# Fused attention and mixture of experts: the experts' slots are chosen beside the token scatters, with early units of 256 rows, three units of 448 rows and another PSUM order

## The chip, the cores and the metric

The kernel runs on one core of a Trainium2 chip. The metric is the device time of one execution in microseconds; three runs of the kernel before took 967.88, 968.69 and 969.49 us, a median of 968.69. The engines are TensorE (PE, with weight loads as PEld), VectorE (DVE), ScalarE (ACT), GpSimd (POOL) and SyncE (SP). Each has its own instruction queue and takes its instructions in order; they meet through semaphores.

## The reference

```python
# attention: q, k, v of 8 batches x 8 heads x 576 rows x 64
scores = scale * q @ k.T
thresh = max(scores) - tau                      # tau = 0.02
scores = where(scores >= thresh, scores, -1e9)
x = softmax(scores) @ v                         # rows: 4608 tokens x 512
# mixture of 8 experts, one expert per token
logits = x @ w_gate
e_idx = argmax(logits)                          # the token's expert
gate_w = softmax(logits)[e_idx]
eom = sigmoid(x @ w_output_gate)
for e in range(8):
    h = maximum(x[e_idx == e] @ w1[e], 0)       # 512 -> 1024
    out[e_idx == e] = gate_w * eom[:, e] * (h @ w2[e])   # 1024 -> 512
```

All of it is float32. The matmuls of the experts are made in three products of halves: each operand is split into a high part and the remainder (xh, xl; w1h, w1l; w2h, w2l; hh, hl), and hi*hi, hi*lo and lo*hi are summed in PSUM.

## The kernel before, in words

**Attention** (class `Attention`) goes through the batches in pairs, software pipelined over steps g. As soon as a pair's rows of x are known, its logits are summed (`logit_sums`) and a generator `Router.route` is put into a queue. `advance`, called in every step, moves that queue on by a piece. `route` takes the argmax, counts the tokens per expert so far by two matmuls (`place`) and scatters each row of 514 numbers (512 of x, the gate and the token's number) with nine indirect DMAs of 128 rows into a DRAM buffer `xs`, where expert e has its region from row e*CAP. The routing of the last pair can only be done when attention has ended, so it lies beside the first expert work. The rows of the first two experts ("early" experts) that come from the earlier pairs (up to `cut`) go into regions of their own of `esize` rows, so that their units can start before the last pair is routed.

**Experts** (class `Experts`) works in units. A unit is a block of rows of one expert, with eight f steps, each of 128 of the 1024 hidden columns. In a step, `first(f)` makes 12 matmuls of 128x128 weights against all the rows of the unit (lines 945 to 947), ACT makes hh (949), DVE makes hl (950), and `second(f)` makes three matmuls of 512 columns per tile of 128 rows, with the hidden rows as the stationary operand (966 to 968), summed over f in one PSUM bank per tile. `run` emits `first` of a step ahead of `second` of the step before. `finish` scales the sums (751) and writes them by indirect DMA to the tokens' rows of the output (752). The next unit's rows are loaded by `gather` from `xs` (908, on SP's queue), and `prep` transposes them by 64x64 pieces (931) and splits them (761, 764), in two calls during the later steps of the unit ahead.

The weights come in quarters of an expert: SP loads two halves of 512 KB per quarter (`load`, 718) into one of RB = 4 raw buffers; `split_until` makes the high half on ACT (761) and the low half on DVE (764), into NW = 4 sets, some steps ahead of their use.

The order of units in `begin` is: two early units of 384 rows; then six units of 512 rows (experts 2 to 7, `Base`), with four units of 256 rows (`Pair`) between them, whose expert and rows come from a table "p" made on DVE in `Router.finish` after all counts are known; and one unit of 128 rows (`Flex`), interleaved into the eleventh unit and the beginning of the last. Behind everything a loop (`rest`) runs a `Flex` unit for each slot of 128 rows that is left, read from a table "s"; on these inputs nothing was left. Altogether the static units have room for 4992 rows.

Slots are filled with whatever lies in `xs`; rows that no token fills must be harmless. So `finish` scatters pad rows (`zrow`) behind each expert's last row with eight indirect DMAs (`pads`), and `init_units` fills other rows with 32 DMAs during attention. The third unit's gather is held until the token scatters and the pads are done.

PSUM has eight banks. When attention ends, the expert part opens three pools over the banks that attention frees: y (4 banks, the sums), x (2, transposes), h (2, hidden).

Of the kernel before, what the change touches and what calls it, by code (L numbers as in the profile page):

```python
# [20 lines left out]
class Attention:  # L21
# [281 lines left out]

    def run(self, hooks):
# [4 lines left out]
        for g in range(G + self.TAIL):  # L309
# [68 lines left out]
class Router:  # L378
    NPAIR = 4

    def __init__(self, ctx, tc, ntok, E, DM, early, esize, cut):
# [12 lines left out]
        self.A = E * self.CAP + 2 * P  # L394
# [9 lines left out]
        self.ecap = c.tile([P, E], F32, name="ecap")  # L404
        self.asc = c.tile([P, E], F32, name="asc")
# [3 lines left out]
        for e in range(E):  # L409
            nc.gpsimd.memset(self.ebase[:, e : e + 1], float(e * self.CAP + self.base[e]))  # L410
            nc.gpsimd.memset(self.elim[:, e : e + 1], float(e * self.CAP + esize) if e < early else -1.0)
# [19 lines left out]
        self.prows = c.tile([1, 2, self.NPAIR], I32, name="pairs")  # L431
        self.total = c.tile([1, 1], I32, name="total")
        self.odd = ctx.enter_context(tc.tile_pool(name="rodd", bufs=1))
        self.ripe = False
# [14 lines left out]
    def init_units(self):  # L449
        E = self.E  # L450
        parts = [(self.xs[self.A :, :], "itok")]
        for e in range(self.early, E + 1):
            n = self.base[e] if e < E else 2 * P
            parts.append((self.xs[e * self.CAP : e * self.CAP + n, :], "itok"))
        for dst, group in parts:
            for r in range(0, dst.shape[0], P):
# [4 lines left out]
                yield None  # L461
# [23 lines left out]
    def route(self, bp, rows, LX):  # L485
# [77 lines left out]
        G.tensor_copy(rows[:, :, self.DM], sc)  # L563
        yield False
# [30 lines left out]
    def finish(self, ctx):  # L595
        nc, E = self.nc, self.E
        sm = ctx.enter_context(self.tc.tile_pool(name="rfin", bufs=1, reuse_waits="tile"))
        V = nc.vector
        pad = sm.tile([P, E], F32, name="padf")
        padi = sm.tile([P, E], I32, name="padi")  # L600
        V.tensor_scalar(pad, self.cnt, self.pid, None, op0=ALU.add)
        V.tensor_copy(padi, pad)
# [6 lines left out]
        row = lambda n, name, dt=F32: sm.tile([1, n], dt, name=name)  # L609
        ni, nj, nf, np, m0, v = row(E, "ni", I32), row(E, "nj", I32), row(E, "nf"), row(E, "np"), row(E, "m0"), row(E, "v")  # L610
        cp, ci, cm = row(E + 1, "cp"), row(E + 1, "ci"), row(E + 1, "cm")
        V.tensor_tensor(nf, self.cnt[0:1], self.ebase[0:1], op=ALU.subtract)
        V.tensor_scalar(nf, nf, float(P - 1), None, op0=ALU.add)
        V.tensor_copy(ni, nf)
        yield False
# [58 lines left out]
class Experts:  # L674
# [102 lines left out]
    def begin(self, nstatic):  # L777
# [6 lines left out]
        for i in range(len(make)):  # L784
            for g in range(4):
                self.seq.append((i, g))
                if i == self.FLEX:
                    self.seq.append((None, g))
# [377 lines left out]
```

## Time and profile before

| | us |
|---|---|
| median of the runs | 968.69 (967.88 to 969.49) |
| the profiled execution | 967.93 |
| its span | 966.2 |
| attention's last matmuls, first expert matmul | 490.43 |
| first matmul of the third unit | 568.63 |
| first matmul of the last unit | 909.49 |
| last matmul | 958.16 |
| mean granted TensorE clock | 0.995 |

The page of the profile gives the busy time of each engine, the span in 40 slices, and the groups of instructions with what they waited for. A stretch's row gives the busy time of each engine in it, the granted clock as a share of full speed, and the share of the DMA engines. In the timeline each matmul stands with its start and its duration; matmuls are pipelined, so that the distance between starts, not the duration, is what one costs.

### The profile page before, as it was taken

To read this page: it belongs to the slowest core of one execution; us is meant where nothing else is said; L and a number is where in the kernel's file an instruction comes from. 1 tells how busy PE (TensorE), PEld (TensorE's weight loads), DVE (VectorE), ACT (ScalarE), POOL (GpSimd) and SP (SyncE) were. 2 spreads that over 40 slices of the span, in tenths; PEclk is the share of its full clock that TensorE was granted. 3 is DMA by queue.
4 is the path that set the end of the run, shared out by engine and by line. 5 is a ranking of instruction groups with operands and counts; after the bars stand their busy time and mean duration, and the time that the engine had idled before them with its cause. 6 is when DMAs were issued, how large, how long until landed. Compare 5 with 4: busy or idle time off the path is not lost. (4 is left out here: it accounts for less than half of the span.)

```text
span 966.2 us, 22101 instructions
## 1 busy us (share of the span) xinstructions
PE 948.4 (98%) x8491; PEld 716.2 (74%) x8491; DVE 690.3 (71%) x1631; ACT 592.3 (61%) x1052; POOL 339.0 (35%) x573
## 2 busy tenths in 40 slices
PE   9999999999999999999989899999999999999996
PEld 5677676776766767667668787778878878878785
DVE  7999999999999999999865752535535535536721
ACT  6888888888879888788853342324424434435521
POOL 4343443656736675466635410202102002002001
PEclk9999999999999999999999999999999999999998
DMA  4355443133331342317157753426526526537401
GB/s 161 102 165 159 147 151 90 57 93 110 122 93 54 115 132 79 93 54 271 60 188 227 252 180 112 150 90 219 192 84 222 167 89 237 166 98 231 152 11 44
DMA packets 87531, 130.88 MB, mean 135 GB/s; under 512 B 24831, under 2 KB 51711, under 8 KB 87424
## 3 DMA queue, kind: packets, MB, share of 16 engines
q1 hardware_dynamic: 62096, 103.70, 34.1%
q0 software_dynamic: 6640, 21.02, 5.7%
q10 hardware_dynamic: 18688, 4.72, 2.0%
q8 instruction: 68, 1.11, 0.5%
q14 instruction: 39, 0.32, 0.1%
HBM read 95.26 MB, written 30.22 MB: 130 GB/s over the span
## 5 line engine op out<-in xcount | busy, mean ns | idle before, releaser
L162 ACT ACTIVATE p<-s,mn 128x576 f32<-128x576 f32 x288 | 207.7, 791 | 43.2 <-DVE s L148 42.4
L148 DVE TENSOR_SCALAR_CACHE_REDUCE s<-ps 128x576 f32<-128x576 f32 x288 | 205.9, 750 | 26.9 <-PE ps L137 26.3
L175 DVE SCALAR_TENSOR_TENSOR p<-s,thr,p 128x576 f32<-128x576 f32 x288 | 223.5, 812 | 0.0
L137 PE MATMUL ps<-qk 64*128 64x288 f32 (+1 forms) x1280 | 181.7, 419 | 0.1
L949 ACT ACTIVATE hh<-ph 128x512 fp32r<-128x512 f32 (+2 forms) x95 | 48.6, 511 | 208.3 <-PE ph L947 204.1
L155 POOL TENSOR_SCALAR thr<-mn,tau_sb 128x2 f32<-128x2 f32 x144 | 107.1, 744 | 194.9 <-DVE s L148 192.5
L752 POOL DMA_INDIRECT out_dram<-yo,kid x39 | 43.0, 1104 | 367.6 <-DVE yo L751 272.3
L950 DVE SCALAR_TENSOR_TENSOR hl<-ph,hh 128x512 fp32r<-128x512 f32 (+2 forms) x95 | 54.9, 578 | 141.2 <-ACT hh L949 141.1
L945 PE MATMUL ph<-xh,w1h 128*128 128x512 f32 (+2 forms) x380 | 134.7, 354 | 0.6 <-ACT xl L330 0.6
L946 PE MATMUL ph<-xl,w1h 128*128 128x512 f32 (+2 forms) x380 | 132.0, 347 | 0.2 <-DVE xl L764 0.2
L947 PE MATMUL ph<-xh,w1l 128*128 128x512 f32 (+2 forms) x380 | 131.9, 347 | 0.0
L966 PE MATMUL py<-w2h,hh 128*128 128x512 f32 x301 | 119.9, 398 | 3.2 <-ACT hh L949 3.2
L968 PE MATMUL py<-w2h,hl 128*128 128x512 f32 x301 | 119.8, 398 | 3.1 <-DVE hl L950 3.1
L137 PEld LDWEIGHTS ps<-qk 64*128 64x128 f32 (+1 forms) x1280 | 107.5, 177 | 18.4 <-DVE s L148 3.7
L967 PE MATMUL py<-w2l,hh 128*128 128x512 f32 x301 | 119.2, 396 | 0.0
L217 PE MATMUL pt<-ident,p 64*128 64x64 f32 x2304 | 100.9, 227 | 0.0
L239 PE MATMUL pa<-PTb,vld 128*64 128x320 f32 x640 | 100.0, 442 | 0.2 <-DMA PTb<-PTc 0.2
L217 PEld LDWEIGHTS pt<-ident,p 64*128 64x128 f32 x2304 | 82.8, 139 | 19.5 <-issue 13.2
L764 DVE TENSOR_TENSOR w1l<-r,w1h 128x1024 fp32r<-128x1024 f32 x52 | 63.6, 1223 | 23.3 <-ACT w1h L761 22.4
L945 PEld LDWEIGHTS ph<-xh,w1h 128*128 128x128 f32 x380 | 71.3, 188 | 11.9 <-ACT xl L330 0.8
L239 PE MATMUL pa<-PTa,vld 128*64 128x256 f32 x640 | 79.7, 387 | 0.2 <-ACT PTb L202 0.2
L946 PEld LDWEIGHTS ph<-xl,w1h 128*128 128x128 f32 x380 | 71.4, 188 | 10.1 <-DVE xl L764 0.6
(221 smaller groups left out, 1502.3 us busy)
## 6 DMA issues: line engine op xcount, KB each, us to landing
r<-in_moe_w_dram SPq DMA_DIRECT2D x104, 512.0 KB, 3.9
qk<-in_qkv_dram SPq DMA_DIRECT2D x31, 608.0 KB, 4.6
vld<-in_qkv_dram SPq DMA_DIRECT2D x32, 320.0 KB, 4.4
xs<-zrow SPq DMA_DIRECT2D x32, 257.0 KB, 2.7
xg<-xs SPq DMA_DIRECT2D x6, 1028.0 KB
PTb<-PTc ACTq DMA_DIRECT2D x16, 288.0 KB, 4.7
xg<-xs SPq DMA_DIRECT2D x4, 514.0 KB, 4.3
xg<-xs SPq DMA_DIRECT2D x2, 771.0 KB
```

Of the source, the lines that this page charges most:

```text
L137: nc.tensor.matmul(ps[a][rows, o : o + HS], q[pp, t * P : t * P + w], k[pp, k0 : k0 + HS], start=True, stop=True)
L148: nc.vector.tensor_scalar(s, ps[a][:, c0 : c0 + S], SC, None, op0=ALU.mult, op1=ALU.min, accum_out=mn[:, a : a + 1])
L162: self.nc.scalar.activation(e, s, AF.Exp, bias=mn[:, a : a + 1], scale=-1.0)
L175: nc.vector.scalar_tensor_tensor(e, s, thr[:, a : a + 1], e, op0=ALU.is_le, op1=ALU.mult, accum_out=acc[:, a : a + 1])
L217: nc.tensor.transpose(pt[:, o : o + 64], p[hs[h], k0 : k0 + P], id_[hs[h], hs[h]])
L239: nc.tensor.matmul(pa[self.half[a], 0:N], vm[:, kb, a], PT[:, 4 * a + kb if i else self.NK - 1], start=(i == 0), stop=(i == self.NB), skip ...
L945: nc.tensor.matmul(ph, w1h[:, c, fs], self.xh[:, c, 0:N], start=(c == 0), stop=False)
L946: nc.tensor.matmul(ph, w1h[:, c, fs], self.xl[:, c, 0:N], start=False, stop=False)
L947: nc.tensor.matmul(ph, w1l[:, c, fs], self.xh[:, c, 0:N], start=False, stop=(c == 3))
L966: nc.tensor.matmul(Y, hh[:, ts], wh, start=(f == 0), stop=False)
L967: nc.tensor.matmul(Y, hh[:, ts], wl, start=False, stop=False)
L968: nc.tensor.matmul(Y, hl[:, ts], wh, start=False, stop=(f == 7))
```

## The change

1. **Early units of 256 rows** in place of 384 (`esize` is 2 * P).
2. **Slots by size.** The units behind the early ones have fixed sizes: SLOTS = 448, 448, 448, 512, 512, 512, 384, 256, 256, 256, 256, worked in the order UNITS. Which expert and which rows a slot takes is chosen at run time by `choose`, slot by slot: the expert with the most rows left among those whose need, padded, lies at or above the slot's size. With the two early ones that is 13 units with room for 4800 rows. `Flex` has no static place any more; `rest` begins its loop at slot 0.
3. **`choose` stands beside the scatters.** It is a generator in a second queue, moved on by `aside` in each f step, 11 small DVE instructions per slot. A unit's weight loads are issued only when its slot is chosen (`known`).
4. **Units of 448 rows are `Turned`**: in `second` the weights are the stationary operand, the rows stream, so the sum is the transpose, 4 blocks of 128 columns x 448 rows. `finish` copies it to SBUF, and `flip` in steps 1 and 2 of the next unit turns it back with 8 transposes of 128x128 each and writes the rows out.
5. **The third unit's gather does not wait for the pads**: rows up to SAFE = 512 of each region are filled in advance (40 DMAs, two per step of the queue), and pads of rows below that are dropped by an index beyond the bounds.
6. The last pair's two logit sums go through the queue (`last_sums`) instead of standing in line; `advance` is called 6 times a step while the last pair is routed, and none at the very first step; one half split fewer is made ahead in unit 0.
7. The PSUM pools are opened in the order y, h, x.

Of the diff, long parts are left out:

```diff
@@ Attention.run
                 if lu == self.nu - 1:
-                    self.logit_sums(0)
-                    self.logit_sums(1)
+                    rt.queue.append(self.last_sums())
@@ Router
-    NPAIR = 4
+    SLOTS = (448, 448, 448, 512, 512, 512, 384, 256, 256, 256, 256)
+    SAFE = 512
...
+    def aside(self, n):
+        for _ in range(n):
+            if self.side and next(self.side[0], self.side) is self.side:
+                self.side.pop(0)
...
         G.tensor_copy(rows[:, :, self.DM], sc)
+        if bp == self.cut + 1:
+            self.side.append(self.choose())
+            self.last = True
         yield False
...
+    def choose(self):
...
+        for k, z in enumerate(self.SLOTS):
+            yield
+            V.scalar_tensor_tensor(key, st[:, 1], float(z), st[:, 0], op0=ALU.is_ge, op1=ALU.mult)
+            V.tensor_reduce(mx, key, axis=AX.X, op=ALU.max)
+            V.scalar_tensor_tensor(cand, key, mx, self.desc[0:1], op0=ALU.is_equal, op1=ALU.mult)
+            V.tensor_reduce(cm, cand, axis=AX.X, op=ALU.max)
+            yield
...
+            self.tables.append(k)
@@ Router.finish
-        V.tensor_copy(padi, pad)
+        V.tensor_tensor(held, pad, self.first, op=ALU.subtract)
+        V.tensor_scalar(held, held, float(self.SAFE), float(1 << 20), op0=ALU.is_lt, op1=ALU.mult)
+        V.tensor_tensor(padi, pad, held, op=ALU.add)
@@ Experts
-    PAIRS = (2, 4, 6, 8)
-    FLEX = 10
+    UNITS = (0, 3, 7, 1, 8, 4, 9, 2, 6, 10, 5)
...
-        for name, bufs in (("y", 4), ("x", 2), ("h", 2)):
+        for name, bufs in (("y", 4), ("h", 2), ("x", 2)):
...
+        make = [lambda e=e: Base(self, e) for e in range(rt.early)]
+        make += [lambda s=s: (Turned if rt.SLOTS[s] % P else Pair)(self, s) for s in self.UNITS]
+        self.known = lambda i: i < rt.early or self.UNITS[i - rt.early] in rt.tables
...
     def load_next(self):
-        if self.nload < len(self.seq):
+        while self.nload < min(len(self.seq), self.nsplit + self.RB):
             i, g = self.seq[self.nload]
+            if not self.known(i):
+                return
@@ Experts.run
-                if i == self.FLEX and f % 2:
-                    self.flex.step(f // 2, self.take())
...
+                if i and f in (1, 2):
+                    self.unit(i - 1).flip(f - 1)
-                self.split_until(2 * self.used + (4 if f % 2 else 3))
+                self.split_until(2 * self.used + (4 if f % 2 else 3) - (i == 0))
...
-                for _ in range(4):
+                for _ in range(6 if rt.last else 3 if i or f else 0):
                     rt.advance(True)
+                rt.aside(1 if rt.tables and i < rt.early else 2 if i else 4)
+                self.load_next()
@@ Pair
+        rt.after(ins, [x for _, x in rt.tok])
+        if self.s == 0:
+            rt.tc.declare_no_dep(ins.ins, group="pad", reason="rows of their own")
+        else:
+            rt.after(ins, rt.pads)
@@ Turned(Pair)
+    def second(self, f):
...
+        for c, Y in enumerate(self.Y):
+            wh, wl = (w[:, f % 2, c * P : c * P + P] for w in (w2h, w2l))
+            nc.tensor.matmul(Y[:, 0:N], wh, hh[:, 0:N], start=(f == 0), stop=False)
+            nc.tensor.matmul(Y[:, 0:N], wh, hl[:, 0:N], start=False, stop=False)
+            nc.tensor.matmul(Y[:, 0:N], wl, hh[:, 0:N], start=False, stop=(f == 7))
...
+    def flip(self, k):
+        ex, nc = self.ex, self.nc
+        for i, pt in enumerate(ex.px()):
+            t = 2 * k + i
+            o = max(0, t * P - 64)
+            for c in range(4):
+                nc.tensor.transpose(pt[:, c * P : c * P + P], self.yt[:, c, o : o + P], ex.ident)
+            ex.emit_out(pt, self.keys, t, slice(0, P if t else 64))
@@ the call
-        rt = Router(ctx, tc, out.shape[0], w1.shape[0], out.shape[1], 2, 3 * P, nbp - 2)
+        rt = Router(ctx, tc, out.shape[0], w1.shape[0], out.shape[1], 2, 2 * P, nbp - 2)
```

On DVE, in the sixth step of unit 0, the kernel before has this order (r are raw weights, w2l and w1l their low halves, xl the rows' low half, padf and padi the pads' indices; the tables come behind):

```order
L950 SCALAR_TENSOR_TENSOR hl<-ph,hh 128x384
L764 TENSOR_TENSOR xl<-px,xh 128x2x3x64 x2
L764 TENSOR_TENSOR w2l<-r_8062,w2h 128x1024
L950 SCALAR_TENSOR_TENSOR hl<-ph,hh 128x384
L764 TENSOR_TENSOR xl<-px,xh 128x2x3x64 x2
L764 TENSOR_TENSOR w1l<-r_8310,w1h 128x1024
L601 TENSOR_SCALAR padf<-pr,pid 128x8
L602 CAST padi<-padf 128x8
L950 SCALAR_TENSOR_TENSOR hl<-ph,hh 128x384
```

The kernel after has, from the same step on (dst and dsti are the last pair's row numbers for the scatters, st, key, cand and got the choice's state):

```order
L978 SCALAR_TENSOR_TENSOR hl<-ph,hh 128x256
L805 TENSOR_TENSOR xl<-px,xh 128x2x2x64 x2
L805 TENSOR_TENSOR w1l<-r_8078,w1h 128x1024
L560 TENSOR_REDUCE dst<-pso 128x9
L576 CAST dsti<-dst 128x9
L623 TENSOR_TENSOR st<-pr,first 1x8
L624 TENSOR_SCALAR st<-st 1x8
L625 TENSOR_SCALAR st<-first 1x8
L626 COPY st<-asc 1x8
L629 SCALAR_TENSOR_TENSOR key<-st 1x8
L630 TENSOR_REDUCE mx<-key 1x1
L631 SCALAR_TENSOR_TENSOR cand<-key,mx,desc 1x8
```

The row numbers stand ahead of these rows in the kernel before (behind the hl of the third step), and behind the split of the sixth step now, with the choice directly after them and ahead of the next hl.

On SP, around the third unit's gather, the kernel before has (r are halves of weights, xg the unit's rows):

```order
L718 DMA r_8809<-in_moe_w_dram 128x4x256 [waits DMAHW2_49,DVE_49]
L908 DMA xg<-xs 128x4x514 [waits DMASW4_49,DMASW3_49,DMASW5_49,DMASW2_49,DMASW6_49,DMASW1_49,DMASW7_49,DMASW0_49,DMAHW3_49,PE_49,Pool_49]
L718 DMA r_8810<-in_moe_w_dram 128x2x512 [waits DMAHW4_49,DVE_49]
L988 TENSOR_LOAD pairs [waits DVE_49]
L988 ISA x2
L718 DMA r_8905<-in_moe_w_dram 128x4x256 [waits DMAHW5_49,DVE_49]
```

The kernel after has there:

```order
L759 DMA r_8855<-in_moe_w_dram 128x4x256 [waits DMAHW4_49,DVE_49]
L1020 TENSOR_LOAD picks
L1020 ISA x2
L759 ISA
L759 DMA r_8856<-in_moe_w_dram 128x2x512 [waits DMAHW5_49,DVE_49]
L1037 ISA
L1037 DMA xg<-xs 128x3x514 [waits DMASW4_49,DMASW3_49,DMASW5_49,DMASW2_49,DMASW6_49,DMASW1_49,DMASW7_49,DMASW0_49,DMAHW6_49,PE_49,Pool_49]
L1037 ISA
L1037 DMA xg<-xs 64x514 [waits DMAHW7_49]
L1037 ISA
L1037 DMA xg<-xs 64x514 [waits DMAHW0_49]
```

The gather is three transfers now (384 rows, and 64 rows twice, once for each half of the partitions), behind weights of a chosen expert, whose loads wait for the table on DVE.

On TensorE, at a step of a unit of 512 rows behind a turned one, the eight transposes stand between two steps of the kernel after:

```order
L996 MATMUL py<-w2h,hl 128x512
L1104 MATMUL px<-ident,rows 128x128 x8
L973 MATMUL ph<-xh,w1h 128x512
L974 MATMUL ph<-xl,w1h 128x512
L975 MATMUL ph<-xh,w1l 128x512
```

The kernel before goes from the second matmuls of one step directly to the first ones of the next there.

## Rows read from the trace of the kernel before

**Rows 1.** The page: the span.

```profile
span 966.2 us, 22101 instructions
```

**Rows 2.** Busy time by stretches: start:end, length, each engine (x instructions), clock, DMA share, GB/s.

```profile
490.43:568.63 78.20, 72.07 (x408) 62.56 (x406) 50.28 (x121) 29.73 (x46) 29.73 (x41) 0.98 0.64 207
568.63:909.49 340.86, 339.66 (x1842) 278.78 (x1840) 166.43 (x207) 138.64 (x211) 37.14 (x49) 1.00 0.50 164
503.20:506.60 3.40, 3.19 (x8) 2.52 (x9) 2.84 (x6) 2.63 (x5) 0.77 (x3) 0.51 0.65 224
514.00:526.00 12.00, 12.00 (x78) 10.21 (x77) 5.29 (x8) 4.65 (x9) 7.82 (x10) 1.00 0.87 281
530.00:545.00 15.00, 14.40 (x74) 12.87 (x72) 10.84 (x49) 3.67 (x6) 10.67 (x11) 1.00 0.87 295
```

**Rows 3.** Waits of TensorE, 490 to 570: total us, times, longest.

```profile
PE py L966 <- ACT hh L949: 3.2, 2, 2.1
PE py L968 <- DVE hl L950: 2.3, 1, 2.3
PE ph L945 <- ACT xl L330: 0.6, 1, 0.6
```

**Rows 4.** Timeline of TensorE, a step's first matmul: start, us, operation.

```profile
511.40 0.34 PE L945 MATMUL ph<-xh,w1h 128*128 128x384 f32 x1
...
515.58 0.34 PE L945 MATMUL ph<-xh,w1h 128*128 128x384 f32 x1
...
590.83 0.40 PE L945 MATMUL ph<-xh,w1h 128*128 128x512 f32 x1
...
596.42 0.40 PE L945 MATMUL ph<-xh,w1h 128*128 128x512 f32 x1
...
670.69 0.28 PE L945 MATMUL ph<-xh,w1h 128*128 128x256 f32 x1
...
673.49 0.28 PE L945 MATMUL ph<-xh,w1h 128*128 128x256 f32 x1
```

**Rows 5.** The same, around units of 256 rows without and with the flexible unit.

```profile
801.04 0.28 PE L945 MATMUL ph<-xh,w1h 128*128 128x256 f32 x1
...
826.61 0.40 PE L945 MATMUL ph<-xh,w1h 128*128 128x512 f32 x1
...
830.79 0.40 PE L945 MATMUL ph<-xh,w1h 128*128 128x512 f32 x1
...
871.14 0.28 PE L945 MATMUL ph<-xh,w1h 128*128 128x256 f32 x1
...
909.49 0.40 PE L945 MATMUL ph<-xh,w1h 128*128 128x512 f32 x1
...
916.42 0.40 PE L945 MATMUL ph<-xh,w1h 128*128 128x512 f32 x1
```

**Rows 6.** Timeline, flexible unit's transposes and the next matmul; then durations (ns) of all four.

```profile
875.74 0.63 PE L1025 MATMUL px<-ident,xgf 128*128 128x128 f32 x4 [0.22 <-DMA xgf<-xs]
876.12 0.37 PE L945 MATMUL ph<-xh,w1h 128*128 128x256 f32 x1
...
L1025 PE MATMUL px<-ident,xgf x4: 272/273/300, 875.7 to 876.1; 128*128 128x128 f32 x4
```

**Rows 7.** Groups on VectorE, 490 to 570: busy us, mean ns, idle before.

```profile
L764 DVE TENSOR_TENSOR w2l<-r,w2h 128x1024 fp32r<-128x1024 f32 x9 | 11.0, 1221 | 1.9 <-ACT w2h L761 1.9
...
L950 DVE SCALAR_TENSOR_TENSOR hl<-ph,hh 128x384 fp32r<-128x384 f32 x15 | 8.3, 552 | 11.9 <-ACT hh L949 11.8
...
L639 DVE TENSOR_TENSOR cp<-cp,np 1x1 f32<-1x1 f32 x8 | 1.2, 147 | 0.2
```

**Rows 8.** Landing of weights; then token scatters and gathers: duration, first and last start.

```profile
DMA to landing us min/median/max: 5.0/5.8/6.5
...
L473 POOL DMA_INDIRECT xs<-rows,dsti x9: 969/977/1889, 511.3 to 522.8; - x9
...
L908 SPq DMA_DIRECT2D xg<-xs x2: 130/248/367, 544.7 to 568.8; - x2
```

More of the change, by code (lines that the diff above doesn't have):

```diff
@@ L302, in logit_sums, with last_sums @@
             rt.queue.append(rt.route(bp, rt.xrows[bp], LX))
+    def last_sums(self):
+        yield True
+        for k in range(2):
+            self.logit_sums(k)
+            yield True
     def run(self, hooks):
@@ L410, in __init__ @@
             nc.gpsimd.memset(self.ebase[:, e : e + 1], float(e * self.CAP + self.base[e]))
+            nc.gpsimd.memset(self.first[:, e : e + 1], float(e * self.CAP + (self.base[e] if e < early else 0)))
             nc.gpsimd.memset(self.elim[:, e : e + 1], float(e * self.CAP + esize) if e < early else -1.0)
@@ L451, in init_units @@
         parts = [(self.xs[self.A :, :], "itok")]
-        for e in range(self.early, E + 1):
-            n = self.base[e] if e < E else 2 * P
-            parts.append((self.xs[e * self.CAP : e * self.CAP + n, :], "itok"))
+        for e in range(E + 1):
+            r0 = e * self.CAP + (self.base[e] if e < self.early else 0)
+            parts.append((self.xs[r0 : r0 + self.SAFE, :], "itok"))
         for dst, group in parts:
@@ L834, in run @@
                     b.w[f // 2] = self.take()
-                if i == self.FLEX + 1 and f == 1:
-                    self.flex.second(turned)
-                    self.flex.finish()
                 if not ahead:
@@ L848, in run @@
                     prev = (b, f)
-                if i == self.FLEX and f % 2:
-                    self.flex.step(f // 2, self.take())
-                if i == self.FLEX + 1 and f == 0:
-                    turned = self.flex.transposed()
                 k = f - (6 if late else 5)
@@ L860, in run @@
                     self.unit(i + 1).gather()
-                if i == self.FLEX - 1 and f == 7:
-                    self.flex.gather()
-                if i == self.FLEX and f == 0:
-                    self.flex.prep()
                 if rt.pending is not None:
@@ L982, in finish @@
             self.ex.emit_out(Y, self.keys, t)
+    def flip(self, k):
+        pass
 def where(ex, table, s):
@@ L993, in __init__ @@
     def __init__(self, ex, s):
-        self.ex, self.nc = ex, ex.nc
-        self.nt = 2
-        assert "p" in ex.rt.tables
-        self.e, self.row = where(ex, ex.rt.prows, s)
-        self.reset()
-    def gather(self):
-        rt = self.ex.rt
-        self.xg = self.ex.gp.tile([P, 4, rt.W], F32, name="xg")
-        src = rt.xs[bass.ds(self.row, self.N), :]
-        ins = self.nc.sync.dma_start(self.xg[:, 0 : self.nt], src.rearrange("(t p) w -> p t w", p=P))
-        rt.after(ins, [x for _, x in rt.tok] + rt.pads)
+        self.ex, self.nc, self.s = ex, ex.nc, s
@@ new lines, in __init__, with load @@
+        rt = ex.rt
+        assert rt.SLOTS[0] <= rt.SAFE
+        self.nt = -(-rt.SLOTS[s] // P)
+        assert s in rt.tables
+        self.e, self.row = where(ex, rt.prows, s)
+        self.reset()
+        self.N = rt.SLOTS[s]
+    def load(self, dst, r0, n):
+        rt = self.ex.rt
+        src = rt.xs[bass.ds(self.row + r0, n), :]
+        ins = self.nc.sync.dma_start(dst, src if n < P else src.rearrange("(t p) w -> p t w", p=P))
+        rt.after(ins, [x for _, x in rt.tok])
[3 more added lines that the diff above has]
+            rt.after(ins, rt.pads)
@@ L1115, in build @@
             ex.run()
-        ex.rest(1)
+        ex.rest()
 def lay_out(q, k, v, wg, wog):
```

149 lines of the change are left out of this document (97 added, 52 removed).

## The prediction

> **What bounds the kernel now.** I read the page first, then the busy time by stretches, then the waits of TensorE, then starts of matmuls in the timeline, and last the scatters and weight loads. The profiled execution took 967.93 us, of which 966.2 are the span [rows 1]; 1.7 us lie around it and stay. The runs shown have a median of 968.69, so I add 0.76 us at the end.
>
> Between the third unit's first matmul (568.63) and the last unit's (909.49) it is busy 339.66 of 340.86 us at full clock [rows 2]: here only a change of its own work counts. The 78.20 us before that, two units of 384 rows beside the routing, are another matter: 72.07 busy, 6.1 idle, and 3.4 us in which the granted clock was 0.51, that is the lower level, 1.2 GHz, right after an idle stretch [rows 2]. The idle time has three names: a second matmul waits for the activation hh (3.2 us) or for the vector engine's hl (2.3), and the first matmul of a unit for xl of the attention, whose bank it takes over (0.6) [rows 3].
>
> One f step, read from the start of its first matmul to the next start of the same line, takes 4.18 us with 384 rows (511.40 to 515.58), 5.59 with 512 and 2.80 with 256 [rows 4]. All three are proportional to the rows, 0.0873 us a row for the eight steps. So a unit of 256 takes 22.4 us, of 384 33.4, of 512 44.7, and one of 448, which no row shows, 39.1 by the same slope. The steady stretch holds five units of 512 and four of 256, 313.2 us; with 12.8 us for the flexible unit (below) that is 326.0 of 340.86, and the 14.9 left over nine unit boundaries are 1.65 us each (the transposes that prepare the next unit's rows).
>
> **The change part by part.**
>
> *Work of TensorE behind the early stretch.* Before: six units of 512, four of 256 and the flexible one of 128 rows. After: three of 448, three of 512, one of 384 and four of 256. Three units of 512 become three of 448 and one of 384: 117.3 + 33.4 - 134.2 = +16.6 us, and one more boundary, +1.65. The flexible unit goes. It ran beside a unit of 256 and the first step of the next one: the unit with it took 38.35 us (871.14 to 909.49), the one without 25.57 (801.04 to 826.61), and the first step behind 6.93 (to 916.42) against 4.18 (to 830.79) [rows 5]. So it costs 12.78 + 2.75 = 15.5 us, and this is gained. Unit 1's last second step, which runs after the third unit's first matmul, shrinks from 9 matmuls of 0.233 us to 6: -0.7.
>
> *The turned units.* In a unit of 448 rows the weights stand still and the rows stream, so the product is transposed and has to be turned back: two groups of eight 128x128 transposes a unit, 48 in all, on TensorE. The nearest row is four of them of the same shape, 0.63 us in the timeline from the first's start to the last's end, but the next matmul starts 0.38 us after the first [rows 6]. So each takes 0.095 us of the queue, a group 0.76, six groups 4.6 us. Bounds: 0.058 us, a matmul of 128 columns by the slope of rows 4 (2.8 in all), and the duration of a single one, 0.273 [rows 6] (13.1). I take 4.6, by the starts: the 24 matmuls of a 512-row step last 0.40 us each and take 0.233 (5.59 / 24) [rows 4], so a duration is no price. The Trainium skill ("TensorE: Matmul & The Clock Gate", Part 4: PE-mode transpose) gives about 275 ns for such a transpose in a kernel; by it the 48 would be 13.2 us, 8.6 more. The durations of the trace agree with the page (273 ns), the starts (95 ns) do not [rows 6]. The copies out of PSUM that precede a turn (four of 448 columns, shared by two engines) and the scaled output rows lie beside matmuls of a step of 2.8 us or more; at nothing.
>
> Sum behind the early stretch: 16.6 + 1.65 - 15.5 - 0.7 + 4.6 = +6.65 us.
>
> *The early stretch, its work.* Two units of 384 become two of 256. The matmuls in it were 2 x 33.4 less the 2.1 us of the last second step, 64.7; after, 44.8 - 1.4 = 43.4. Two boundaries are 3.3 in both. What is left of the 78.20 before is 10.2: 6.1 idle [rows 3], 1.6 lost to the lower clock (half of 3.19 busy) [rows 2], and 2.5 of the attention's last matmuls and small things, which stay. The question is what stands in the place of the 7.7.
>
> *(a) The table beside the scatters.* The choice of the experts is taken out of the finish and put on the vector engine earlier: 4 + 11 small operations fall into one step of unit 0, more later in portions of four. A small operation costs 0.147 us and with the gap 0.175 [rows 7], so 15 are 2.6 us. A step of 256 rows is 2.80 us; a weight split (1.22) and hl (at most 0.55, the row for 384) fill 1.77 of it [rows 4, 7]. 1.0 us hides some of the chain, 1.6 us shows as a wait for hl. Bounds 0 (the hidden layer is two tiles deep) and 2.6. Later portions of four, 0.7 us, fit into the 1.0. The two sums of the last logits (queued, not in line) go behind a split instead of ahead of it; at nothing, up to 1.6 us either way.
>
> *(b) Releases late beside scatters.* The matmul that waited for hh in the pad scatters is one of the two in [rows 3]; scatters now last as long beside shorter steps. Bounds 0 and 4, I take 1.0.
>
> *(c) The rows of the third unit.* Before, its gather waited for tokens and pads and was issued at 544.7 [rows 8]; the third unit began at 568.63, so nothing waited. Now only the token scatters hold it. They were issued from 511.3 to 522.8 [rows 8]; the row numbers that feed them stand three steps later now, at the end of the sixth, which at 2.80 us a step with the waits of (a) and (b) is again about 511, so I leave them there, and add about 5 us to land (weights landed in 5.0 to 6.5 [rows 8]): 528. Both early units are 128 rows shorter, and TensorE wants the rows in unit 1's seventh step: 490.43 + 2.5 (attention) + 2.6 (a, b) + 1.65 + 14 steps of 2.80 less the lag of one second step, 1.4, so 535.0. In the queue ahead of the gather are weight halves: faster units want about eight of 0.52 MB from 511 to 528, 4.2 MB, beside 2.4 MB of tokens; at the 281 GB/s seen beside the token scatters [rows 2] 17 us move 4.8 MB, so 1.8 MB is left over. With the gather's 0.9 MB, and 730 pad rows of 2 KB (1.5 MB) in the same time, 4.2 MB at 295 GB/s (seen beside the pads [rows 2]) take 14 us: 542. Without the pads, 9 us: 537. Landing as fast as a weight (5.0) gives 533, no wait. I take 540.5, 5.5 us late; bounds 0 and 13 (6.5 to land, behind 14 of backlog).
>
> *(d)* After a wait of some us the clock fell for 3.4 us before [rows 2]; half of that price, 0.8, since the wait is cut by the preparing transposes; bounds 0 and 1.65.
>
> *PSUM in another order, zero rows in advance, one half split fewer ahead in unit 0.* The first takes the wait of 0.6 away, which is counted in the 6.1; if the first matmul of unit 0 then waits for another bank, it is the 0.6 again. The zero fill and its eight more transfers run in the attention, where TensorE is the bound, at nothing. The split is taken out of a vector engine that has 1.0 us to spare a step; it would cost 1.2 once.
>
> Early stretch after: 43.4 + 3.3 + 2.5 + 1.6 + 1.0 + 5.5 + 0.8 = 58.1, against 78.20: -20.1. With +6.65: -13.4, so 954.5 us for a profiled execution, 955.3 as a median.
>
> **The rivals.**
>
> 1. *The rows come in time.* The gather of 0.9 MB need not wait until the halves issued ahead of it are done. For it: weights land within 6.5 us even at the share of 0.87 [rows 2, 8]. Against it: three transfers behind the weights in one queue order, and pads beginning as the gather does. (c) and (d) go: 949.0.
>
> 2. *The transfers starve the early units.* The same 4 MB of weights are wanted in two thirds of the time. For it: the share of 0.87 in both scatter windows [rows 2]. Then (c) is 13, (d) 1.65 and weights are late too, (b) 1 more: 955.3 + 7.5 + 0.85 + 1 = about 964.6.
>
> 3. *Each turn costs its whole duration.* If nothing overlaps a transpose, as where each waits for a copy out of its bank, 48 x 0.273 are 13.1 in place of 4.6: 963.8. For it: the durations; against it the starts [rows 6].
>
> 4. *Slower: rows are left over.* The new slots are sized to the experts' counts, and nothing runs the flexible unit statically any more: the loop behind the units begins at zero. If one row of any expert is uncovered, one pass runs with nothing beside it: a gather (5.0), eight halves of 0.52 MB at 295 GB/s (14.2), the last two splits (2.4), and an output of 5: +27, so 982, slower than before. It decides from one uncovered row. From the reference's inputs the counts are 619, 496, 677, 491, 670, 499, 508 and 648; less the early units' 256 for experts 0 and 1 they fit the slots (expert 6, 508 in 512, is the closest: four rows to spare). Against it, then, the count; for it, that four rows is little and rounding of near ties moves tokens.
>
> **How the numbers follow.** The forecast, rows 2 to 10 us late and all else as above: 0.52, 955.3. Rival 1: 0.22. Rival 2: 0.13. Rival 3: 0.05. Rival 4: 0.08. Two runs of this kernel can be told apart from about 0.2%, 1.9 us, so "the same" is 966.8 to 970.6. Faster: 0.52 + 0.22 + 0.05 and 0.10 of rival 2, 0.89; the same 0.03, the rest of rival 2; slower 0.08. The range 947.0 to 965.0 holds the forecast with its bounds, rival 1 down to (a) and (b) at nothing (946.4 is its end), rival 3, and half of rival 2.
>
> **What would show it.** A step of 448 rows takes 4.89 us from start to start, a group of eight turns 0.76 before the next matmul; the third unit starts at about 548.5; TensorE has one wait of some 5 us ahead of it for the third unit's rows, and a lower clock behind it; the loop behind the units does not run. It would be wrong if steps of 448 rows are longer than 5.0, if turned rows hold TensorE up because their copies come late, if waits for weights (through hh, hl or splits) stand in the third to fifth unit, or if the last matmul is followed by loads.

## The result, and the profile after

The changed kernel takes 953.94 us in the median (952.99 to 956.26, four runs) against 968.76 of the kernel before; the ratio is 0.9851 (0.9831 to 0.9871). The profiled execution took 953.54 us, its span 951.5. The first expert matmul stands at 489.58 us, the third unit's first matmul at 547.54.

The stretches of TensorE's work answer to [rows 2] (start:end, length, busy time of each engine, granted clock, DMA share, GB/s):

```profile
489.58:547.54 57.96, 51.97 (x350) 44.25 (x348) 42.24 (x113) 27.65 (x48) 33.54 (x40) 0.94 0.74 248
547.54:951.50 403.96, 396.86 (x2194) 341.10 (x2190) 207.22 (x356) 156.62 (x249) 50.66 (x57) 1.00 0.45 147
...
526.00:540.00 14.00, 10.07 (x65) 8.68 (x65) 7.93 (x23) 4.35 (x7) 11.26 (x10) 1.00 1.05 369
...
540.00:547.00 7.00, 6.72 (x34) 5.20 (x33) 3.05 (x9) 2.31 (x6) 1.59 (x4) 0.51 0.53 158
```

The early stretch is 57.96 us where it was 78.20: -20.2. From the third unit on it is 403.96 us where it was 397.57 (568.63 to 966.2): +6.4. The first expert matmul comes 0.85 us sooner. Together -14.7, the difference of the spans. In the last row of the fence the granted clock is 0.51, the lower level, 1.2 GHz, for 7 us: 6.72 us of busy TensorE at half clock are 3.3 us lost. The stretch before it has the highest share of the DMA engines in these rows, 1.05.

TensorE's waits between 480 and 620 answer to [rows 3] (total us, times, longest):

```profile
PE px L1067 <- DMA xg<-xs: 3.9, 1, 3.9
PE py L996 <- DVE hl L978: 1.0, 2, 0.7
PE ph L975 <- DVE w1l L805: 0.8, 1, 0.8
```

Of the three waits of before, those for hh and for the attention's xl are gone, and the one for hl is down from 2.3 to 1.0 us. In their place are one of 0.8 us for the low half of a weight (w1l) and one of 3.9 us for the third unit's rows, ahead of the lower clock. In the timeline it stands at the transposes, with the time waited at the row's end:

```profile
539.89 0.73 PE L1067 MATMUL px<-ident,xg 64*128 64x64 f32 x12 [3.93 <-DMA xg<-xs]
```

The steps of 448 rows and a group of turns answer to [rows 4] and [rows 6]; the last line has the durations of all 48 turns:

```profile
566.78 0.36 PE L973 MATMUL ph<-xh,w1h 128*128 128x448 f32 x1
...
571.68 0.36 PE L973 MATMUL ph<-xh,w1h 128*128 128x448 f32 x1
...
598.85 1.03 PE L1104 MATMUL px<-ident,rows 128*128 128x128 f32 x8
599.64 0.48 PE L973 MATMUL ph<-xh,w1h 128*128 128x512 f32 x1
```

```profile
L1104 PE MATMUL px<-ident,rows x48: 270/272/273, 598.9 to 851.3; 128*128 128x128 f32 x48
```

A step takes 4.90 us; eight turns take 0.79 us from their first start to the next matmul's, although a single one lasts 0.27.

What the third unit's rows waited for, on POOL (durations, first and last start) and in SP's queue, answers to [rows 8]:

```profile
L487 POOL DMA_INDIRECT xs<-rows,dsti x9: 967/1438/1983, 512.4 to 525.8; - x9
L487 POOL DMA_INDIRECT xs<-zrow,padi x8: 967/968/1237, 531.4 to 540.6; - x8
```

```profile
SPq L1037 <- DMA xs<-rows,dsti: 3.6, 1, 3.6
```

```profile
534.28 1.32 SPq L1037 DMA_DIRECT2D xg<-xs  x3
```

The nine token scatters are issued from 512.4 to 525.8, 1.67 us apart (before 1.44). SP's queue then waits 3.6 us for them to land, starts the gather at 534.28, and TensorE has the rows at 539.89.

### The profile page after: what moved, and what is told of

It reads as the page before. It is cut to its first block, busy times and chain, and to the rows that moved or that the text cites. A ratio compares the mean times of both kernels' runs of the same rounds, so it can differ in the third digit from the quotient of the medians.

```text
span 951.5 us, 22606 instructions
## 1 busy us (share of the span) xinstructions
PE 936.8 (98%) x8571; PEld 721.5 (76%) x8571; DVE 705.4 (74%) x1752; ACT 594.5 (62%) x1074; POOL 349.8 (37%) x581
## 3 DMA queue, kind: packets, MB, share of 16 engines
q8 instruction: 68, 1.11, 0.5%
## 5 line engine op out<-in xcount | busy, mean ns | idle before, releaser
L977 ACT ACTIVATE hh<-ph 128x256 fp32r<-128x256 f32 (+3 forms) x103 | 49.6, 482 | 184.0 <-PE ph L975 175.9
L973 PE MATMUL ph<-xh,w1h 128*128 128x256 f32 (+3 forms) x412 | 140.3, 340 | 0.0
L975 PE MATMUL ph<-xh,w1l 128*128 128x256 f32 (+3 forms) x412 | 137.2, 333 | 0.8 <-DVE w1l L805 0.8
L974 PE MATMUL ph<-xl,w1h 128*128 128x256 f32 (+3 forms) x412 | 137.3, 333 | 0.2 <-DVE xl L805 0.2
L978 DVE SCALAR_TENSOR_TENSOR hl<-ph,hh 128x256 fp32r<-128x256 f32 (+3 forms) x103 | 55.6, 539 | 102.0 <-ACT hh L977 101.3
L996 PE MATMUL py<-w2h,hl 128*128 128x512 f32 x214 | 85.2, 398 | 1.0 <-DVE hl L978 1.0
L994 PE MATMUL py<-w2h,hh 128*128 128x512 f32 x214 | 85.0, 397 | 0.0
L995 PE MATMUL py<-w2l,hh 128*128 128x512 f32 x214 | 84.8, 396 | 0.0
L973 PEld LDWEIGHTS ph<-xh,w1h 128*128 128x128 f32 x412 | 77.9, 189 | 8.9
L975 PEld LDWEIGHTS ph<-xh,w1l 128*128 128x128 f32 x412 | 78.0, 189 | 6.8 <-DVE w1l L805 1.0
```

The lines of the kernel that those rows point to most:

```text
L973: nc.tensor.matmul(ph, w1h[:, c, fs], self.xh[:, c, 0:N], start=(c == 0), stop=False)
L974: nc.tensor.matmul(ph, w1h[:, c, fs], self.xl[:, c, 0:N], start=False, stop=False)
L975: nc.tensor.matmul(ph, w1l[:, c, fs], self.xh[:, c, 0:N], start=False, stop=(c == 3))
L994: nc.tensor.matmul(Y, hh[:, ts], wh, start=(f == 0), stop=False)
L996: nc.tensor.matmul(Y, hl[:, ts], wh, start=False, stop=(f == 7))
```

## The experiments

All are edits of the changed kernel unless a line says otherwise. Kernels under one heading ran in turns on one chip; times are compared within a heading.

### What the rows' lateness costs, and what sets it

**The third unit reads rows that are there** (early_rows).

```diff
-        src = rt.xs[bass.ds(self.row + r0, n), :]
+        src = rt.xs[bass.ds(self.row + r0, n), :] if self.s else rt.xs[rt.A + r0 : rt.A + r0 + n, :]
-        rt.after(ins, [x for _, x in rt.tok])
+        rt.after(ins, [x for g, x in rt.tok if self.s or g == "A"])
         if self.s == 0:
+            rt.tc.declare_no_dep(ins.ins, group="tok", reason="rows of their own")
```

> The third unit reads its 448 rows from the early experts' region, which is complete long before, in place of its own rows; all else as in the changed kernel, so it no longer waits for the last tokens (its results are those of other rows). Theory 1 (the rows' lateness costs what the trace shows: 3.9 us of wait and about 3.5 us of lower clock behind it): the wait for xg is gone, the clock stays full, 953.9 - 7.4 = about 946.5 us. Rival (something else is due at the same point, the weights of the chosen experts or the splits): another wait of 2 us or more appears between 530 and 550, and the time is 950 or more.

Measured: 951.45 us, ratio 0.9816 (0.9797 to 0.9835). The rival is nearer: 2.7 us below gather_first, which ran beside it and is as long as the changed kernel. TensorE's new wait, then the transposes of the third unit's rows and ACT's copy of them in the timeline, and the pad scatters (durations, first and last start):

```profile
PE px L1068 <- issue: 3.5, 1, 3.5
```

```profile
536.09 0.65 PE L1068 MATMUL px<-ident,xg 64*128 64x64 f32 x14
...
541.85 1.09 ACT L802 CAST xh<-px 128x384 fp32r<-128x384 f32 x4 [6.66 <-remote]
```

```profile
L487 POOL DMA_INDIRECT xs<-zrow,padi x8: 972/974/1216, 531.6 to 540.8; - x8
```

The wait for the rows is gone, but another one of 3.5 us has come, named "issue", with no releaser. ACT waits 6.7 us for a hand-off ("remote", one for which the trace has no releaser) in the same place. The transposes that it copies end at 536.7, so 5.1 us of that are late; it goes on at 541.85, as the last pad scatter's issue ends (540.8 and 1.0), and TensorE 1.5 us behind it. This stand is called a freeze below. The trace names neither the weights nor the splits, which the rival had in mind.

**The gather ahead of the weights in SP's queue** (gather_first).

```diff
-                if not final and f == late:
+                if not final and f == (1 if late else 0):
```

> The third unit's gather is put three steps earlier into SP's queue (step 1 of unit 1, not 4), so weight loads queue behind it while it waits for the tokens. Theory 2 (the scatters and the gather land late because weight halves fill the DMA engines): the tokens land 3 us or more earlier than 533, the rows are there before 537, and the time falls to 947 to 951 us. Rival (the scatters land when POOL has issued them, whatever else moves): the gather starts at 532 or later as it did at 534.3, and the weights that were held back cost 0 to 4 us: 953 to 958.

Measured: 954.16 us, ratio 0.9848 (0.9830 to 0.9867), no difference. SP's wait, the token scatters, the gathers, and TensorE's wait:

```profile
SPq L1037 <- DMA xs<-rows,dsti: 7.9, 1, 7.9
```

```profile
L487 POOL DMA_INDIRECT xs<-rows,dsti x9: 967/1452/1982, 512.5 to 525.8; - x9
```

```profile
L1037 SPq DMA_DIRECT2D xg<-xs x4: 373/396/479, 533.7 to 557.0; - x4
```

```profile
PE px L1067 <- DMA xg<-xs: 5.0, 2, 3.1
```

SP stood 7.9 us at the gather and issued no weights; the tokens were issued at the same times, and the gather started at 533.7, 0.6 us sooner, as the rival had it. So the halves that were held back don't set when the tokens land. From the last scatter's start to the gather's it is about 8 us in both. Theory 2 as a whole is not refuted by this: the halves issued before the gather were still on their way. A row of the stretch in which SP stood:

```profile
525.00:532.00 7.00, 7.00 (x49) 6.42 (x48) 6.02 (x18) 2.76 (x5) 5.78 (x5) 1.00 1.03 369
```

The share of the DMA engines is 1.03 all the same, and from 526 to 531 the queue of plain transfers (q1 of the DMA view) moves 1.11 MB beside the tokens.

**Early units of 384 rows, the same number of rows in all** (early384).

```diff
-    SLOTS = (448, 448, 448, 512, 512, 512, 384, 256, 256, 256, 256)
+    SLOTS = (448, 448, 448, 512, 512, 512, 256, 256, 256, 256, 128)
-    UNITS = (0, 3, 7, 1, 8, 4, 9, 2, 6, 10, 5)
+    UNITS = (0, 3, 6, 1, 7, 4, 10, 2, 8, 5, 9)
-        rt = Router(..., 2, 2 * P, nbp - 2)
+        rt = Router(..., 2, 3 * P, nbp - 2)
```

> Early units of 384 rows as before, with slots 448 x 3, 512 x 3, 256 x 4 and 128, so again 13 units and 4800 rows: the same work for TensorE, only more of it ahead of the third unit. Theory 1 (the changed kernel's early stretch loses time because 256 rows are too few to cover the routing): the third unit's rows are there in time, no wait and no lower clock, 946 to 948 us. Rival (the waits for hh and hl of the kernel before belong to the routing beside 384 rows and come back): 5 to 7 us of waits between 495 and 555, 952 to 955 us.

Measured: 957.16 us, ratio 0.9874 (0.9851 to 0.9897), 3.0 us above gather_first beside it, and above the rival's range. The rows are in time, and still it is slower. The profiled execution took 961.86 us, the longest of the four (the others 956.04 to 958.21), so what its trace shows is more than the median has. In the timeline, a step's last first matmul, ACT's hidden tile of that step, and the last pad scatter; then two stretches:

```profile
544.21 0.33 PE L975 MATMUL ph<-xh,w1l 128*128 128x384 f32 x1
```

```profile
549.25 0.49 ACT L977 ACTIVATE hh<-ph 128x384 fp32r<-128x384 f32 x1 [12.94 <-remote]
```

```profile
547.65 0.97 POOL L487 DMA_INDIRECT xs<-zrow,padi  x1 [0.30 <-issue]
```

```profile
534.00:549.00 15.00, 7.85 (x37) 6.24 (x35) 3.23 (x14) 1.43 (x2) 11.54 (x11) 0.89 0.85 276
549.00:556.00 7.00, 6.21 (x17) 5.34 (x18) 4.20 (x11) 2.85 (x4) 0.00 (x0) 0.51 0.38 130
```

The matmul ends at 544.5, and ACT starts only at 549.25; it has had no hand-off ("remote") for 12.9 us. TensorE is busy 7.85 of 15 us, and the 7 us after that go at the lower clock. The stand ends 0.6 us after the last pad scatter's issue. The freeze of early_rows is here at its longest. Between 536 and 549 the trace has no packet in a queue that loads instructions, so no instruction load that the trace shows ended the stand.

**512 rows in place of 448** (all512).

```diff
-    SLOTS = (448, 448, 448, 512, 512, 512, 384, 256, 256, 256, 256)
+    SLOTS = (512, 512, 512, 512, 512, 512, 384, 256, 256, 256, 256)
```

> Slots of 512 rows in place of the three of 448, so no turned units. By the steps' slope 3 x 64 rows x 0.0873 = +16.8 us, less six groups of turns at 0.79 and their neighbours, -5.2: 953.9 + 11.6 = about 965.5 us. Rival (turned units cost more than the turns that the trace shows, as by copies out of PSUM): less than +9, 960 to 962.5.

Measured: 966.40 us, ratio 0.9970 (0.9958 to 0.9983), 12.2 us above gather_first beside it, where 11.6 was expected. The slope and the price of the turns hold for 448 rows; most of the change's gain is in these three units.

### Whether the pad rows cause the freeze

**768 rows filled in advance** (fill768), and the same with the third unit reading early rows (rows768).

```diff
-            parts.append((self.xs[r0 : r0 + self.SAFE, :], "itok"))
+            parts.append((self.xs[r0 : r0 + (768 if e < E else self.SAFE), :], "itok"))
-        V.tensor_scalar(held, held, float(self.SAFE), float(1 << 20), ...)
+        V.tensor_scalar(held, held, 768.0, float(1 << 20), ...)
```

> 768 rows of each expert's region are filled in advance (58 transfers in attention, not 40), and pads below that are dropped: eight pad scatters are still issued, but only some 75 rows of 1024 are written, not 730. Theory 3 (the pad rows' writes make the third unit's rows and the engines' hand-offs late): the rows land by 537, TensorE's wait of 3.9 us is under 1.5, and the time is 946 to 950 us. Rival (the tokens and the weights alone make them late, or it is the issuing of the scatters): the wait stays at 3 us or more and the time at 952.5 to 955.5.

> The third unit reads 448 rows of the early experts' region (its results are those of other rows), and 768 rows of each region are filled in advance. With only the first of the two, 951.5 us, TensorE stood 3.5 us beside the pads for no wait that the profile names. Theory 3: that stand is gone too, 946 to 948 us, which is then what all lateness at this place costs. Rival (it is not the pad rows): it stays, 950.5 to 952.5.

Measured: 953.02 us, ratio 0.9887 (0.9873 to 0.9901), and 947.18 us, ratio 0.9827 (0.9813 to 0.9841). With 768 rows filled the wait for the rows stays. TensorE's wait, and the token scatters:

```profile
PE px L1067 <- DMA xg<-xs: 4.5, 1, 4.5
```

```profile
L487 POOL DMA_INDIRECT xs<-rows,dsti x9: 967/1437/1976, 513.6 to 527.0; - x9
```

So pad rows don't make the rows late; the rival holds there. This trace has the landing of the gather's first transfer, 6.1 us after its issue. With early rows as well, TensorE has no wait over 1 us left; the longest:

```profile
PE py L996 <- DVE hl L978: 1.0, 2, 0.7
```

The two differ by 5.8 us, which is what the lateness of the rows costs where no freeze takes its place.

**Pads later** (pads_later), and with early units of 384 rows (pads_later384, with the edit of early384).

```diff
-                if not rt.queue and not fin:
+                if not rt.queue and not fin and i >= 2:
-                if not final and f == late:
+                if not final and f == (3 if i == 2 else late):
```

> The pad scatters are issued in the third unit's steps 1 and 2, when its rows are already there, and the fourth unit's gather in step 3 instead of 0. Theory 3: the wait for the third unit's rows shrinks to under 1.5 us as in the kernel with 768 rows filled; the engines' hand-offs can be late beside the pads in the third unit instead, 947 to 952 us. Rival (pads have no part in it): the rows still land at about 540 and nothing is gained, 953 to 956.

> The same pads, but with early units of 384 rows (slots 448 x 3, 512 x 3, 256 x 4, 128). Theory 3: the 11 us for which ACT, DVE and TensorE stood beside the pads in the kernel with 384 rows are gone in that place; the stand moves to the third unit or vanishes, 946 to 952 us. Rival: the stand belongs to that point of the program (a weight, an instruction load), not to the pads, and stays: 956 to 958.

Measured: 957.97 us, ratio 0.9937 (0.9924 to 0.9951), and 955.20 us, ratio 0.9909 (0.9895 to 0.9924): 5.0 and 2.2 us above fill768 beside them, and in neither case within a range that was expected. Waits of TensorE of the first, then of the second:

```profile
PE px L1067 <- DMA xg<-xs: 4.5, 1, 4.5
PE px L959 <- DMA xg<-xs: 2.9, 1, 2.9
```

```profile
PE px L959 <- DMA xg<-xs: 3.7, 1, 3.7
```

In both the fourth unit's gather, which waits for the pads, now comes late (2.9 and 3.7 us): the price of where I put them. The rows of the third unit came no sooner in the first, again against theory 3. In the second the freeze of early384 is gone from its place, and none has come beside the pads in their new one: they start from 572.9 to 582.9, and TensorE has no wait beside them.

These traces also hold the landings of the token scatters. Two rows of the first kernel, for scatters issued between 511 and 516 and between 523 and 527, with the median time from issue to landing:

```profile
xs<-rows,dsti POOLq DMA_INDIRECT x2, 3.0
```

```profile
xs<-rows,dsti POOLq DMA_INDIRECT x4, 8.1
```

So the first scatters landed after 3.0 us and the later ones after 8.1, without a pad beside them. The share of the DMA engines was 0.20 from 513 to 516 and 1.05 from 524 to 531.

### The chain made shorter, and the PSUM order

**The changed kernel again** (after_again), no edit.

> The changed kernel itself, so that the three others are compared with it on one chip. Its ratio to the kernel before was 0.985 (0.983 to 0.987); if the chip alone set the 964.4 us of the kernel before beside the last four kernels, the ratio here is the same; if the kernel before varies by itself, 0.984 to 0.990.

Measured: 954.07 us, ratio 0.9862 (0.9837 to 0.9886); the kernel before took 968.17 us beside it, on the chip on which it took 964.44 beside the four kernels above. So the kernel before varies by itself from one series to the next; whether the others move with it was not measured, and only kernels of one series are set against each other here.

**The routing sooner** (fill768_adv4, with the edit of fill768).

```diff
-                for _ in range(6 if rt.last else 3 if i or f else 0):
+                for _ in range(6 if rt.last else 4):
```

> 768 rows of each region are filled in advance, and the routing's queue is moved on four times in every step from unit 0's first step on, as in the kernel before, not three times and none in the first: the last pair's row numbers are made at the end of the fourth step, not the sixth. Theory 4 (the lateness is set by the chain row numbers, nine scatters, landing, gather, landing, and by nothing beside it): scatters start at 507, the rows land at 535, no wait for xg, no lower clock: 5 to 7 us less than the changed kernel beside it. Rival (the vector engine's work in the first steps makes TensorE wait there, as before the change): waits for hh and hl of 2 to 5 us before 510, gain 0 to 3.

Measured: 958.49 us, ratio 0.9902 (0.9875 to 0.9929), with single runs from 954.3 to 967.8; the profiled one is the longest. Its waits of TensorE, and the token scatters:

```profile
PE py L996 <- DVE hl L978: 5.7, 3, 2.4
PE px L1067 <- DMA xg<-xs: 4.3, 1, 4.3
```

```profile
L487 POOL DMA_INDIRECT xs<-rows,dsti x9: 971/971/1087, 510.4 to 520.9; - x9
```

The scatters start 2.4 us sooner than in after_again beside it (512.8), not 5. TensorE pays with 5.7 us of waits for hl. The rival had such waits, but all of them before 510 (1.8 us of them are) and with a gain of 0 to 3; the kernel is 4.4 us slower than after_again. In this execution, some 9 us longer than the median, SP's queue reached the gather only at 545, behind weight loads that waited for VectorE, so here the earlier tokens gave nothing; theory 4 itself is not tested by it.

**Early units of 384 rows with 768 rows filled** (fill768_384, both edits).

> 768 rows filled in advance and early units of 384 rows (slots 448 x 3, 512 x 3, 256 x 4, 128). Theory 4 with theory 3: the rows are there 20 us before they are wanted, and nothing stands beside the few pad rows: 5 to 7 us less than the changed kernel beside it. Rival (the stand of 11 us with 384 rows had to do with this order of units, not with the pads): 0 to 3 us more than the changed kernel.

Measured: 956.84 us, ratio 0.9895 (0.9870 to 0.9921), 2.8 us above the changed kernel beside it: the rival's number. The profiled execution, 954.41 us, is the shortest of the five. A step's last first matmul and TensorE's next one, ACT's hidden tile of that step, and the pad scatters:

```profile
549.17 0.34 PE L975 MATMUL ph<-xh,w1l 128*128 128x384 f32 x1
551.88 0.50 PE L994 MATMUL py<-w2h,hh 128*128 128x512 f32 x1 [2.37 <-ACT hh L977]
```

```profile
551.34 0.49 ACT L977 ACTIVATE hh<-ph 128x384 fp32r<-128x384 f32 x1 [7.44 <-remote]
```

```profile
L487 POOL DMA_INDIRECT xs<-zrow,padi x8: 972/973/1525, 539.0 to 548.9; - x8
```

Only some 75 rows were written by these eight scatters, and ACT still waited 7.4 us for a hand-off. Most of that is the step's own work: the matmul ends at 549.5, ACT starts 1.8 us later, and TensorE loses 2.4 us. So a short freeze comes with next to no rows written, and rows written are not all of its cause. How much they add can't be told from this pair, a longest execution (early384) and a shortest one. The issuing of the scatters itself is left, but rows768 issued them at the same place without a freeze, and pads_later384 at another.

Nor need the freeze be what 384 rows cost. The first matmul of the experts here and in after_again, two steps of the slot of 128 rows, which only the kernels with 384 rows have, and two stretches in which a kernel with 384 rows waited for nothing over 0.4 us (pads_later384 from its first expert matmul to its third unit, this kernel from there on):

```profile
491.73 0.44 PE L973 MATMUL ps<-xh,w1h 128*128 128x384 f32 x1
```

```profile
489.97 0.39 PE L973 MATMUL ps<-xh,w1h 128*128 128x256 f32 x1
```

```profile
794.33 0.22 PE L973 MATMUL ph<-xh,w1h 128*128 128x128 f32 x1
...
796.36 0.22 PE L973 MATMUL ph<-xh,w1h 128*128 128x128 f32 x1
```

```profile
491.81:561.33 69.52, 69.52 (x403) 61.57 (x401) 45.87 (x110) 29.66 (x48) 22.53 (x33) 1.00 0.55 182
```

```profile
565.58:952.60 387.02, 379.91 (x2132) 326.19 (x2129) 203.46 (x356) 153.05 (x248) 48.07 (x56) 0.99 0.46 151
```

The experts begin 1.8 us later (491.7 to 491.8 in the three edits with 384 rows, 489.6 to 490.9 in the changed kernel and its edits with 256). A step of 128 rows takes 2.03 us, where the slope of the prediction gives 1.40; over eight steps that is 5.1 us, of which a part is gained back elsewhere. The two stretches are 456.5 us together; rows768, with 256 rows, needs 454.5 from its first expert matmul (489.90) to its end (944.4). So by an estimate from these rows the kernels with 384 rows would be 3 to 4 us slower without any wait; 2.8 and 3.0 were measured.

**PSUM order undone** (psum_yxh).

```diff
-        for name, bufs in (("y", 4), ("h", 2), ("x", 2)):
+        for name, bufs in (("y", 4), ("x", 2), ("h", 2)):
```

> Only the PSUM pools' order is undone (y, x, h). Theory: TensorE waits 0.6 us for the attention's copy xl at unit 0's second step as in the kernel before, +0.3 to +0.8 us against the changed kernel beside it. Rival (what is gained there is lost at the wait for the third unit's rows, which land when they land): no difference, -0.3 to +0.3.

Measured: 954.37 us, ratio 0.9867 (0.9842 to 0.9892), 0.3 us above after_again, a difference that both expectations allow and that the runs (953.36 to 955.25 against 953.38 to 954.43) can't tell from none. The wait of before is back,

```profile
PE ph L973 <- ACT xl L336: 0.6, 1, 0.6
```

and in exchange the 0.8 us for w1l is gone.

## Why the prediction was right

| term | predicted | trace |
|---|---|---|
| later units | +6.65 | +6.4 |
| step of 448 rows | 4.89 | 4.90 |
| eight turns | 0.76 | 0.79 |
| early stretch | -20.1 | -20.2 |
| (a), (b): hl and weights | 2.6 | 1.0 + 0.8 |
| (c): third unit's rows | 5.5 | 3.9 |
| (d): lower clock | 0.8 | 3.3 |
| third unit's first matmul | 548.5 | 547.5 |

**The later units** came out in their sum, and in the two terms that were looked at, the step of 448 rows and the turns; all512 confirms these from the other side (12.2 us measured, 11.6 by the slope). The slope is not general, though: a step of 128 rows, which the change does not have, takes 2.03 us and not 1.40 (fill768_384). Rival 3 is out: turns cost their starts. Rival 4 did not happen: from the last matmul's start (944.25) to the end it is 7.3 us, where it was 8.0.

**The early stretch** has the right sum of partly wrong terms. Step (c) had the rows at 540.5 and they came at 539.9, but not by the chain that I gave. I had the tokens landed at 528 and the gather behind a backlog of weights and pads for 9 to 14 us. In the trace the last scatter starts at 525.8, 3.0 us later than the step left it, SP starts the gather that waits for them only at 534.3, and the gather takes 5.6 us (6.1 to landing in fill768). The two errors, 6 us too early and 7 us too long, cancel: that the wait came out near 5.5 us is luck. fill768 shows that the pad rows did not have the part that the step gave them. For the weights gather_first shows it only of the halves that were held back; earlier ones were on their way while the tokens landed, and what these cost was not tested.

Step (d) is the term that was mis-sized: the price was right for a wait like the one of before, but here 7.0 us went at the lower clock, 3.3 us lost against 0.8, and I had halved the price for a reason that no row showed. (a), (b) and (c) together were too dear by as much (8.1 against 5.7), so the sum held, again by luck.

Step (b) named a real thing, hand-offs that come late beside scatters, and gave it 1 us. In the changed kernel ACT waits for one too, in the same place:

```profile
ACT xh L802 <- remote: 7.7, 1, 7.7
```

It costs TensorE nothing that its list of waits shows, since the engines wait for the rows at that time anyway; where the rows are in time it costs 3.5 us (early_rows), and with 384 rows from 2.4 us (fill768_384) to 7.8 (early384's longest execution). That is where the forecast of a kernel without the wait would have failed.

**What gives the gain.** Fewer rows in the 448-row units: 12.2 us. Early units of 256 rows, with the slots that go with them: about 3 us (early384 3.0 above gather_first, fill768_384 2.8 above after_again). The rows are as many, but by the traces the difference can lie in the later start of the experts and the dear slot of 128 rows; that a shorter freeze gives it is not shown. The PSUM order: nothing that these runs can tell. What the third unit's gather gains by not waiting for the pads was not tried.

Rival 1 did not come about, since the rows were 3.9 us late; nor did rival 2, since no weight was waited for longer than 0.8 us.

**Open.** Why a freeze comes beside pad scatters in some of these kernels and not in rows768 or pads_later384 I could not settle. Nor is it settled why the later token scatters take 7 to 8 us to land and the first 3: the DMA engines are loaded by the weights and by the tokens themselves, and in every kernel here weights were on their way beside most of the tokens. None of the variants beats the changed kernel with the reference's rows; rows768 shows that 5.8 us would be to be had if the rows were in time without a freeze.

## What to carry to other kernels

Work of a bound engine can be priced by the distance between starts of the same line, and such a price can be carried between shapes that were measured (448 rows, between 384 and 512), but not beyond them (128 rows). A wait that ends at the right time need not have the cause that was written down: hold back the suspected traffic for once and see whether the time of landing moves, and look whether the traffic was really gone. When two kernels differ, compare where each stands before the place of interest too. Taking away the last wait at a crowded place first shows what it covered, so try it with the next suspect taken away as well.

## What the runs showed of the hardware

- Beside back-to-back indirect scatters ACT waited up to 12.9 us for a hand-off, 4.7 us of it behind the end of the last matmul of its step (early384); in early_rows it was 5.1 us behind. In these two it went on within 1 us of the last scatter's end, in fill768_384, where some 75 rows of 1024 were written, 1.5 us after it and 1.8 us behind the matmul. In rows768 and pads_later384 it did not happen.
- A wait of 3.9 us was followed by 7 us at the lower clock level, 3.3 us lost, nearly as much as the wait.
- From the start of the last token scatter to the gather that waits for all of them it is 7.8 to 8.5 us in six kernels (the changed one twice, gather_first, all512, fill768, pads_later, psum_yxh), with weights on their way in each. The first scatters of pads_later landed 3.0 us after their issue, at a share of the DMA engines of 0.20; four later ones after 8.1, at 1.05.
- A step of 128 rows took 2.03 us, one of 256 took 2.80: 0.63 us more than by the slope that holds from 256 to 512 rows.
